# Softmax work of late batches spread over the slots, and third blocks added on TensorE, in an attention and highway kernel

## Chip, cores, metric

The kernel runs on one core of one Trainium2 chip. The metric is device time of one execution in microseconds (us). Every ratio below is the mean time of one kernel's fast runs over the mean of the other kernel's fast runs of the same rounds, with a 95% interval, so it is not quite the ratio of the medians quoted beside it.

## The reference

Linear attention for 8 batches of 8 heads, 576 rows, 64 columns; its result, as 4608 rows of 512, goes through one highway layer.

```python
q_s = softmax(q, axis=-1)              # per row
k_s = softmax(k, axis=2)               # per column
kv  = einsum('bhsd,bhse->bhde', k_s, v)
x   = einsum('bhsd,bhde->bhse', q_s, kv)   # then (4608, 512)
H = maximum(x @ w_h, 0)
T = 1 / (1 + exp(-(x @ w_t + b_t)))
out = T * H + (1 - T) * x
```

## The kernel before

Each piece of work is a small function, and a table of places (`at(place, ...)`) gives the order in which they are issued; batch c's slot has the places 8c to 8c+8. In before engines are seen to keep that order: at 67.45 us x waits 1.13 us for a query copy whose input was ready, because the copy stands behind a sum of 1.34 us on VectorE. The pieces that matter (cut):

```python
def exp_half(b, which, a):   # ScalarE: exponential of half the heads of k or q
    nc.scalar.activation(dst[b][:, :, 2*a:2*a+2, :], in32[which][b]..., AF.Exp)
def cast_v(b, a, eng=None):  # GpSimd: values to 16 bit
def q_sums(b, a):            # VectorE: row sums of half the heads, 1.34 us
def q_scale_p(b, n0, n1):    # GpSimd: queries times reciprocal of the sum
def q_trans(b, g, home=None):     # TensorE turns a third of the queries (one
    ...                           # PSUM buffer, tag "q1"); VectorE copies them
    nc.vector.tensor_copy(qsT[b][:, :, n0:n1, :], t[:, :, 0:w, :])
turned = (6, 7)              # the queries of these are turned by DMA instead
def x_pair(b, a, ...):       # TensorE: x of two of four blocks; ScalarE casts it
def gate(c, ob):             # TensorE: 4 matmuls of 512 columns, ScalarE: tanh
def carry(c, ob):            # TensorE: the same with w_h; VectorE: difference
def blend(c, ob):            # VectorE: (tanh + 1) * difference -> g

added = lambda g: ((0, 1), (0, 1, 2), (0, 1, 2), (0, 1, 2, 3))[g]
def add_x(c, ob):            # g += x for the blocks in `added`
    late = ob == (3 if c == B - 1 else 2) and c % 2 and c < B
    eng = nc.vector if late else nc.gpsimd
    eng.tensor_add(gv(ob), gv(ob), xv(ob))
def turn_block(t, k_, xs, us):   # TensorE turns g back to rows; where x was
    if xs is not None:           # not added, it is accumulated here
        mm(dst, xs, ident, True, False)
    mm(dst, us, ident, xs is None, True)
```

The pieces of softmax, kv and x of a batch b have places around `p = 8 * (b - 1)`, in slot b-1 or the one before, so that they hide between the products of batch b-1. In what follows a query turn is TensorE's transpose of a third of a batch's queries, a query copy is VectorE's copy of it out of PSUM, an x copy is ScalarE's cast of x, an output block is what `turn_block` makes, and an output copy takes it out of PSUM.

The softmax here doesn't subtract the row's maximum and nothing guards it: scores larger than these inputs give would overflow.

## Time and profile before

| | before |
|---|---|
| median of the first 3 runs | 130.17 us (129.74 to 130.88) |
| span of the profiled run | 129.5 us |
| TensorE / VectorE / ScalarE / GpSimd busy | 111.3 / 99.5 / 92.2 / 77.9 us |
| slots 3 to 7 | 13.53, 12.19, 11.81, 10.48, 8.27 us |
| first gate product after slot 7 to start of last output copy ("tail") | 12.32 us |
| start of last output copy to end of span ("end") | 4.01 us |

A slot's length is the distance between the first gate products of two following batches in the timeline. Spans are printed to 0.1 us, so an end is good to about 0.05 us. Two lines of the page of before also belong here: the clock granted to TensorE in 40 slices (9 is full speed), and the queue that brings instructions (packets, MB, share).

```profile
PEclk9999999999999999999999999999999999999998
q8 instruction: 10, 0.16, 0.5%
```

### The profile page before, as it was taken

What the parts mean: (1) busy time and instruction counts of PE and PEld (TensorE: products, weight loads), DVE (VectorE), ACT (ScalarE), POOL (GpSimd) and SP (SyncE); (2) the same over time, 40 slices, a digit from 0 to 9 for tenths busy, and PEclk for the clock granted to TensorE, in tenths of its full rate; (3) what the DMA queues carried; (4) which work ended last, traced back from release to release, by engine and by line L of the source; (5) the groups of instructions that cost most, each with busy time, mean ns of one, the idle gap of its engine ahead of it and who ended that gap; (6) DMA issues with size and microseconds to landing.
All of it is one profiled execution on the core that took longest, in us unless ns stands there. A gap on an engine that the chain in (4) does not pass through costs nothing.

```text
span 129.5 us, 3346 instructions
## 1 busy us (share of the span) xinstructions
PE 111.3 (86%) x1359; PEld 60.8 (47%) x1359; DVE 99.5 (77%) x181; ACT 92.2 (71%) x130; POOL 77.9 (60%) x73
## 2 busy tenths in 40 slices
PE   4978996986967899899769999995989999999940
PEld 2335442353424446455534555454435445579830
DVE  1297356799799999898789998983999656688960
ACT  3553049994996779679929995998797575757640
POOL 2003446690099999839964993699399746434510
PEclk9999999999999999999999999999999999999998
DMA  4999999999999999999999699999406906134994
GB/s 127 365 374 369 401 401 411 411 411 411 405 411 411 402 411 412 405 411 400 305 411 416 258 252 402 405 323 305 167 1 131 363 15 258 71 139 200 395 402 165
DMA packets 20583, 41.24 MB, mean 318 GB/s; under 512 B 5460, under 2 KB 5976, under 8 KB 19544
## 3 DMA queue, kind: packets, MB, share of 16 engines
q1 hardware_dynamic: 20568, 41.03, 85.2%
q8 instruction: 10, 0.16, 0.5%
q14 instruction: 5, 0.04, 0.1%
HBM read 30.41 MB, written 9.44 MB: 308 GB/s over the span
## 4 chain that ended last, share of the span: by engine, by line
PE 25%; DMA 20%; POOL 19%; DVE 17%; issue 7%; SPq 6%; ACT 2%; POOLq 0%; DVEq 0%; ACTq 0%
DMA v<-in_v_dram 12%; POOL eq L264 10%; DMA w32h<-in_moe_w_h_dram 8%; PE pt L64 8%; PE ph L64 8%; DVE r L234 6%; POOL v L195 4%; POOL g L421 4%; PE nat L64 4%; SPq L96 4%; DVE g L409 3%; DVE dd L401 2%; SPq L111 2%; PE psk L64 2%; PE pq L69 2%
## 5 line engine op out<-in xcount | busy, mean ns | idle before, releaser
L64 PE MATMUL pt<-xT,w16t 128*128 128x512 f16 x128 | 33.6, 379 | 2.9 <-DVE dd L401 2.1
L264 POOL TENSOR_TENSOR eq<-eq,r 128x1024 f16<-128x1024 f16 (+2 forms) x16 | 30.1, 1898 | 10.1 <-DVE r L252 10.1
L64 PE MATMUL ph<-xT,w16h 128*128 128x512 f16 x128 | 33.4, 381 | 1.3 <-ACT w16h L116 0.9
L383 ACT ACTIVATE pt<-pt,bt 128x512 f32<-128x512 f32 (+1 forms) x40 | 24.7, 621 | 7.4 <-PE pt L64 7.4
L421 POOL TENSOR_TENSOR g<-g,xT 128x512 f16<-128x512 f16 x21 | 23.9, 1151 | 8.0 <-DVE g L409 8.0
L409 DVE SCALAR_TENSOR_TENSOR g<-pt,dd 128x512 f16<-128x512 f32 (+1 forms) x40 | 25.2, 633 | 2.9
L401 DVE SCALAR_TENSOR_TENSOR dd<-xT,ph 128x512 f16<-128x512 f16 x32 | 21.7, 678 | 4.3 <-PE ph L64 4.2
L64 PEld LDWEIGHTS <-w16t 128*128 128x128 f16 x160 | 14.7, 97 | 19.1 <-issue 6.6
L183 ACT ACTIVATE eq<-q 128x1152 f16<-128x1152 f32 x16 | 18.2, 1176 | 5.4 <-DMA q<-in_q_dram 5.4
L183 ACT ACTIVATE ek<-k 128x1152 f16<-128x1152 f32 x16 | 18.6, 1175 | 1.8 <-DMA k<-in_k_dram 1.8
L195 POOL CAST v<-v 128x1152 f16<-128x1152 f32 x12 | 13.5, 1145 | 10.2 <-DMA v<-in_v_dram 10.2
L64 PEld LDWEIGHTS <-w16h 128*128 128x128 f16 x160 | 13.6, 98 | 11.7 <-ACT w16h L116 2.7
L234 DVE TENSOR_REDUCE r<-eq 128x18 f32<-128x1152 f16 x12 | 16.0, 1344 | 3.9 <-ACT eq L183 3.9
L64 PE MATMUL nat<-ident,g 128*128 128x128 f16 x142 | 16.0, 220 | 0.7 <-DVE g L409 0.4
L64 PEld LDWEIGHTS <-g 128*128 128x128 f16 x144 | 12.5, 98 | 7.6 <-DVE g L409 1.1
L461 ACT COPY o<-nat 128x512 f32<-128x512 f32 x26 | 15.6, 601 | 0.0
L354 ACT CAST xT<-px 128x1024 f16<-128x1024 f32 x10 | 10.2, 1016 | 7.6 <-PE px L64 7.6
L64 PE MATMUL warm<-wide,ident 128*128 128x512 f16 x41 | 11.9, 435 | 1.8 <-DVE wide L153 1.8
L69 PE MATMUL pq<-ident,eq 128*128 128x128 f16 x104 | 8.5, 220 | 2.7 <-DVE qsT L282 1.1
L282 DVE COPY qsT<-pq 128x1024 f16<-128x1024 f16 (+1 forms) x16 | 9.3, 587 | 1.1 <-PE pq L69 0.7
L69 PEld LDWEIGHTS <-eq 128*128 128x128 f16 x108 | 6.9, 98 | 6.0 <-issue 1.9
L357 ACT CAST xT<-px 128x512 f16<-128x512 f32 x8 | 4.3, 590 | 7.4 <-PE px L64 7.4
(57 smaller groups left out, 107.8 us busy)
## 6 DMA issues: line engine op xcount, KB each, us to landing
out_dram<-o SPq DMA_DIRECT2D x8, 1024.0 KB, 4.7
q<-in_q_dram SPq DMA_DIRECT2D x7, 1152.0 KB, 14.2
k<-in_k_dram SPq DMA_DIRECT2D x7, 1152.0 KB, 13.2
v<-in_v_dram SPq DMA_DIRECT2D x5, 1152.0 KB, 13.7
v<-in_v_dram SPq DMA_DIRECT2D x6, 576.0 KB, 11.7
q<-in_q_dram SPq DMA_DIRECT2D x2, 576.0 KB, 4.1
k<-in_k_dram SPq DMA_DIRECT2D x2, 576.0 KB, 7.2
w32t<-in_moe_w_t_dram SPq DMA_DIRECT2D x1, 1024.0 KB, 11.5
```

The lines of the kernel that those rows point to most:

```text
L64: mm = lambda o, l, r, st, sp: nc.tensor.matmul(o, l, r, start=st, stop=sp, skip_group_check=True)
L69: nc.tensor.matmul(o, i, ident, is_transpose=True, start=True, stop=True, skip_group_check=True,)
L183: nc.scalar.activation(dst[b][:, :, 2 * a : 2 * a + 2, :], in32[which][b][:, 2 * a : 2 * a + 2].rearrange("p c n d -> p n c d"), AF.Exp,)
L195: (eng or nc.gpsimd).tensor_copy(o, i)
L234: nc.vector.reduce_sum(qsum[b][:, :, h], eq[b][:, :, h, :], axis=AX.X)
L264: nc.gpsimd.tensor_mul(e, e, r.broadcast_to(list(e.shape)))
L354: copy[how](dst, t2.rearrange("p c (n d) -> p c n d", d=64))
L383: nc.scalar.activation(ps, ps, AF.Tanh, bias=bt2[:, ob : ob + 1], scale=0.5)
L401: nc.vector.scalar_tensor_tensor(dd, xv(ob), -0.5, ps, op0=ALU.mult, op1=ALU.max)
L409: nc.vector.scalar_tensor_tensor(gv(ob), th, 1.0, dd, op0=ALU.add, op1=ALU.mult)
L421: eng.tensor_add(gv(ob), gv(ob), xv(ob))
L461: nc.scalar.copy(o, flat(t))
```

## The change

The intent is to take sums and turns out of the stretch where TensorE waits for them. The query exponentials and sums of batch 5 are issued 2.3 to 3.2 places earlier, between the copies of the queries of the batch before, those of batches 6 and 7 0.2 to 1.6 places earlier; the turns of batch 5 start at the head of their slot; from batch 4 on the two halves of the values are cast one right behind the other; kv of batch 4 moves behind the last turn of its queries; the key exponentials of batch 4 come 1.3 places earlier. The third blocks of batches 2 to 5 are no longer added by GpSimd and VectorE but accumulated on TensorE, and the last addition of batch 7 goes to GpSimd.

```diff
-    added = lambda g: ((0, 1), (0, 1, 2), (0, 1, 2), (0, 1, 2, 3))[g]
+    added = lambda g: ((0, 1), (0, 1), (0, 1), (0, 1, 2, 3))[g]
...
-        late = ob == (3 if c == B - 1 else 2) and c % 2 and c < B
-        eng = nc.vector if late else nc.gpsimd
-        eng.tensor_add(gv(ob), gv(ob), xv(ob))
+        nc.gpsimd.tensor_add(gv(ob), gv(ob), xv(ob))
...
-                5: (-5, -4, -3.4, -2.7, -2.6),
-                6: (-6, -5, -3.95, -3.1, -3),
-                7: (-6, -5, -3.95, -3.1, -3),
-            }.get(b, (-5, -4, -3.9, -2.9, -2.8))
+                5: (-7.5, -6.3, -6.6, -5.5, -5.4),
+            }.get(b, (-6.6, -5.2, -5.5, -3.95, -3.9))
...
-            at(p + sc + (0.6 if b > 5 else 0), E(q_scale_p, b, 4, N9))
-            s = p + {3: 0, 4: 0}.get(b, -0.5)
-            at(s, E(exp_half, b, "k", 0), E(cast_v, b, 0))
-            at(s + 0.9, E(cast_v, b, 1))
+            at(p + sc + (0.5 if b > 5 else 0), E(q_scale_p, b, 4, N9))
+            s = p + {3: 0, 4: -1.3}.get(b, -0.5)
+            at(s, E(exp_half, b, "k", 0))
             at(s + 1, E(exp_half, b, "k", 1))
+            s = p + {3: 0, 4: 0.05, 5: 0.1}.get(b, -0.9)
+            at(s, E(cast_v, b, 0))
+            at(s + (0.9 if b == 3 else 0), E(cast_v, b, 1))
...
-            4: ((3, 4, 4.9), (4.5, 4.5), (5.9, 6.9)),
-        }.get(b, ((2, 3, 4), (4, 4), (5, 6)))
+            4: ((3, 4, 4.9), (4.95, 4.95), (5.9, 6.9)),
+        }.get(b, ((0.5, 1.6, 2.5), (4, 4), (5, 6)))
```

(The five numbers are the places of the two query exponentials, the two half sums and the scaling; then those of the three turns, of kv and of x.)

## The prediction

> **What bounds the kernel now.** I read the page first, then the list of waits, then the timeline in order, and from the built programs which instruction each wait belongs to. A slot c is the stretch in which TensorE makes the gate and carry products of batch c, four of each; softmax, kv and x of batch c+1 are woven in. Before the slots and at the end nothing is reordered except one addition, so the argument needs slots 3 to 7.
>
> ```profile
> PE 111.3 (86%) x1359; PEld 60.8 (47%) x1359; DVE 99.5 (77%) x181; ACT 92.2 (71%) x130; POOL 77.9 (60%) x73
> POOL eq L264 <- DVE r L252: 10.1, 5, 3.2
> PE psk L64 <- POOL v L195: 2.1, 4, 0.7
> PE pq L69 <- DVE qsT L282: 1.1, 3, 0.7
> ```
>
> TensorE is the fullest engine; the next lines (waiter, releaser, total us, times, longest) show its small holes: the kv sums wait for the cast values, query turns for copies on VectorE. GpSimd's 10.1 us waiting for reciprocals says that the sums come late, not that they bound.
>
> The timeline (start, duration, engine, line, what, count, idle before and its end) gives the first gate product of batches 3 to 8 at 56.89, 70.42, 82.61, 94.42, 104.90 and 113.17. So slots 3 to 7 take 13.53, 12.19, 11.81, 10.48 and 8.27 us. TensorE's own work, from starts in the timeline: four matmuls of 512 columns 0.86, an output block 0.28 (five 128-column ones) or 0.34 (six), all turns of one batch 1.0, kv 0.78, x with its ninth rows 0.80. Slot 3: 8x0.86 + 4x0.34 + 1.0 + 0.78 + 0.80 = 10.8, so 2.7 us are holes. The same sum leaves 1.6 in slot 4, 2.2 in slot 5, 0.9 in slot 6 (their output blocks have mostly five matmuls): 7.4 us in all could be had.
>
> ```profile
> 55.97 0.59 ACT L461 COPY o<-nat 128x512 f32<-128x512 f32 x1
> 56.45 1.02 ACT L354 CAST xT<-px 128x1024 f16<-128x1024 f32 x1
> 56.89 1.22 PE L64 MATMUL pt<-xT,w16t 128*128 128x512 f16 x4
> 58.15 0.66 ACT L383 ACTIVATE pt<-pt,bt 128x512 f32<-128x512 f32 x1 [0.68 <-PE pt L64]
> 59.21 2.22 ACT L183 ACTIVATE ek<-k 128x1152 f16<-128x1152 f32 x2
> ...
> 62.47 2.23 POOL L195 CAST v<-v 128x1152 f16<-128x1152 f32 x2
> ...
> 64.76 0.48 PE L64 MATMUL psk<-v,ek 64*64 64x65 f16 x36 [0.61 <-POOL v L195]
> ...
> 65.85 1.34 DVE L234 TENSOR_REDUCE r<-eq 128x18 f32<-128x1152 f16 x1
> ...
> 67.45 0.22 PE L64 MATMUL px_l<-qsT,kvn 64*64 64x64 f16 x2 [1.13 <-DVE qsT L282]
> ...
> 70.24 1.77 DVE L421 TENSOR_TENSOR g<-g,xT 128x512 f16<-128x512 f16 x1
> ```
>
> Here one sees slot 3: the second x copy starts the instant the output copy lets ScalarE go, and the gate waits for it alone; the key exponentials follow; later kv waits for values, x for a query copy that sits behind a sum; and the addition on VectorE takes 1.77 us.
>
> [...] at 67.45 x waits 1.13 us because a short copy stands behind a 1.34 us sum. [...] the addition took 1.77 and 0.77 us beside GpSimd's scaling and 0.42 us near the end, without it. [...] The query turns share one buffer, so each waits for the copy of the one before, which the 1.1 us above shows.
>
> **The change, part by part.**
>
> *Additions.* Third-block additions of batches 2 to 5 leave: two on GpSimd (1.15 each, off the path), two on VectorE (1.77 and 0.77). TensorE gets 16 more 128-column matmuls at 0.056: 0.9 us, of which 0.22 falls in slot 7, which has no holes to hide it. The last addition of batch 7 moves from VectorE to GpSimd:
>
> ```profile
> 114.16 0.69 DVE L409 SCALAR_TENSOR_TENSOR g<-pt,dd 128x512 f16<-128x512 f32 x1
> ...
> 114.89 0.42 DVE L421 TENSOR_TENSOR g<-g,xT 128x512 f16<-128x512 f16 x1
> ...
> 115.37 0.23 PE L64 MATMUL nat<-ident,g 128*128 128x128 f16 x1 [0.28 <-DVE g L421]
> ```
>
> TensorE waits for exactly this one. On GpSimd: 114.85 + 0.1 to start + 1.15 + 0.05 = 116.15 instead of 115.37, **+0.78**, with full TensorE work behind it until 121.
>
> *Slot 3.* I walk the new order with the old durations, as starts follow each other: exponential 1.06, x copy 0.90, tanh 0.58, output copy 0.48, half sum 1.26 (result visible after 1.34), reciprocal 0.30, carry difference 0.60, blend 0.61, query copy 0.60 (visible after 0.69); a product's end is seen 1.07 after its start. ScalarE now has a key exponential of batch 4 ahead of the second x copy: exponential 56.45, x copy 57.51, seen 58.53. The gate's last two matmuls go at 58.58 instead of 57.52: **first hole, 1.06 us**. ScalarE goes on: other key half 58.41, tanh 59.47, output 60.05, query exponentials of batch 5 at 60.53 and 61.59, the first seen at 61.72. VectorE has carry difference at 60.42, then must wait for that: half sum 61.77, blend 63.03, half sum 63.64, reciprocal 64.95, difference 65.25, first query copy of batch 4 at 65.85, seen 66.54. TensorE reached the second turn at 64.2 and has one buffer: it goes at 66.59, **second hole, 2.4**. It then waits for the second copy (67.2, seen 67.89): third turn 67.93, **third hole, 0.9**. kv starts 68.04; its norm is seen at 69.6; carry to 69.71; x starts 69.71 instead of 67.45; gate of batch 4 at 72.6 instead of 70.42. The values, cast by 64.70, no longer matter. With a 0.3 wait on an output copy the holes sum to 4.7: slot 3 takes 15.7, **+2.2**.
>
> *Slot 4.* The turns of batch 5 come early, their scaling (recip 65.25, GpSimd free 65.85, done 70.1) is long over, kv finds its values. Work 10.8 as in slot 3, plus 0.3 for an x copy and little else: 11.2, **-1.0**.
>
> *Slot 5.* Work 8x0.86 + 4x0.34 + 0.78 + 0.80 = 9.8. Holes: 0.3 for an x copy; ScalarE does two exponentials between tanh and output copy, so an output block waits 0.7; a half sum stands before the blend and norm: 0.3. 11.2, **-0.6**.
>
> *Slot 6.* An addition now stands between the halves of the last scaling: values of batch 7 are cast about 1 us later in the slot, kv waits 0.5: 10.7, **+0.2**. *Slot 7*: 0.22 more, **+0.2**.
>
> Sum: +2.2 - 1.0 - 0.6 + 0.2 + 0.2 + 0.78 = +1.8, that is 132.0.
>
> **The rivals.** (a) The change does what it intends: sums and turns leave the critical stretch, the value waits go. For it: 7.4 us of holes, 2.5 us off VectorE. If slot 3 fell to 11.5 as well, the sum would be 1.8 - 4.2, so about 127.8. Against it: [...] the order puts a sum that is not needed until slot 4 before products needed now. (b) The late slots tighten more than I walked: were slots 4 to 7 free of holes, 2.7 us less, 129.2; for it, half of my holes there are of 0.3 us, within the error of a walk. (c) The delay feeds itself: everything after slot 3 starts 2 us later, transposes through DMA of batch 7 start behind the later scaling, and x of slot 6 waits for them; before, they ended close to use. This would add about 1, 133. (d) A load that comes late for the earlier exponentials: batch 5's queries were issued at 40.64; with the page's median 14.2 us to landing that is 54.8, 5 us ahead of use. It is hidden.
>
> **Range and chances.** The program decides the order and the durations are measured, so I hold to the mechanism of slot 3, but small errors of a hand walk lean to (b), and a change made to a tuned kernel was made for a reason; I take 0.6 off: **131.4 us**. Range 129.4, near (b), to 133.0, (c). Faster by over 2% needs 127.6, only (a) in full: 0.07. Slower by over 2% needs 132.8: 0.14. Within 2%: 0.79.
>
> **What would show it.** Right: the gate of batch 3 with about 1 us between its second and third matmul, waiting for the x copy; in slot 3 waits of turns for query copies of about 3 us in all; first gate of batch 4 near 72.6; no kv wait for cast values in slots 3 to 5; slots 4 and 5 about 11.2 each; near the end a wait of an output block for GpSimd's addition of about 1 us. Wrong: first gate of batch 4 before 71, or VectorE's half sum of batch 5 starting before 61, which would mean that ScalarE is not the queue that holds it.

## The result, and the profile after

The changed kernel took 136.16 us (135.46 to 137.09, 4 runs), before 130.52 us (129.74 to 131.08, 4 runs): ratio 1.0441, interval 1.0345 to 1.0537. It is slower by over 4%; the prediction had given slower by over 2% a chance of 0.14, and the time lies above its range.

The page of the profile after, with the lines that answer to those of before (busy times, clock, instruction queue):

```profile
span 135.2 us, 3375 instructions
PE 114.3 (85%) x1375; PEld 62.2 (46%) x1375; DVE 97.9 (72%) x178; ACT 92.1 (68%) x130; POOL 75.7 (56%) x72
PEclk9999999999999999999856999999999999999995
q8 instruction: 11, 0.18, 0.5%
```

VectorE and GpSimd have less to do, as intended. Two things are new: the clock digits 8, 5, 6 in the middle, where slot 3 lies, and an eleventh packet of instructions. The time went to these places (each from the timelines of the two profiled runs):

| stretch | before | after | difference | predicted |
|---|---|---|---|---|
| up to slot 3 | 56.89 | 56.46 | -0.43 | 0 |
| slot 3 | 13.53 | 18.52 | +4.99 | +2.2 |
| slot 4 | 12.19 | 11.38 | -0.81 | -1.0 |
| slot 5 | 11.81 | 11.30 | -0.51 | -0.6 |
| slot 6 | 10.48 | 10.56 | +0.08 | +0.2 |
| slot 7 | 8.27 | 8.44 | +0.17 | +0.2 |
| tail | 12.32 | 13.08 | +0.76 | +0.78 |
| end | 4.01 | 5.46 | +1.45 | 0 |
| sum | 129.5 | 135.2 | +5.7 | +1.8 |

Slot 3 after, in the timeline (start, duration, engine, line, what, count, idle before and its end):

```profile
57.97 1.19 ACT L183 ACTIVATE ek<-k 128x1152 f16<-128x1152 f32 x1
58.14 0.59 PE L64 MATMUL pt<-xT,w16t 128*128 128x512 f16 x2 [1.09 <-ACT xT L354]
...
61.31 1.35 DVE L234 TENSOR_REDUCE r<-eq 128x18 f32<-128x1152 f16 x1 [0.65 <-ACT eq L183]
...
66.12 0.72 PE L69 MATMUL pq<-ident,eq 128*128 128x128 f16 x8 [2.18 <-DVE qsT L282]
67.63 0.37 PE L69 MATMUL pq<-ident,eq 128*128 128x128 f16 x2 [0.78 <-DVE qsT L282]
...
69.07 1.89 PE L64 MATMUL ph<-xT,w16h 128*128 128x512 f16 x4
...
71.56 1.88 PE L64 MATMUL pt<-xT,w16t 128*128 128x512 f16 x4
```

The first five lines are the three holes that the prediction had walked: 1.09, 2.18 and 0.78 us, with the causes it named. The last two are not in it: four matmuls of 512 columns take 1.89 us and not 1.03. The windows view says why (us, then busy time and count of TensorE, its weight loads, VectorE, ScalarE and GpSimd, then granted clock, DMA share, GB/s):

```profile
63.07:66.48 3.41, 1.08 (x15) 0.73 (x13) 3.38 (x6) 1.49 (x3) 3.41 (x4) 1.00 0.91 284
...
64.00:66.00 2.00, 0.00 (x0) 0.00 (x0) 1.97 (x5) 0.56 (x1) 2.00 (x3) 1.00 0.87 299
66.50:68.00 1.50, 0.72 (x11) 0.36 (x11) 0.86 (x2) 0.00 (x0) 1.50 (x2) 0.50 1.05 412
68.00:70.00 2.00, 2.00 (x76) 1.38 (x76) 0.90 (x3) 0.00 (x0) 2.00 (x2) 0.50 1.04 411
70.00:72.00 2.00, 2.00 (x13) 0.45 (x12) 0.91 (x2) 0.32 (x1) 2.00 (x3) 0.50 1.04 410
72.00:73.20 1.20, 1.20 (x4) 0.42 (x3) 0.48 (x1) 0.70 (x1) 0.89 (x1) 0.50 1.03 407
```

The clock was halved (0.50) from about 66.5 to 73.3 us, 6.8 us, right after the hole of 2.18 us. No stretch of full idleness as long as 3.41 us came before it: TensorE was still 1.08 us busy in the 3.41 us before the fall. How much idleness it took in the traces is said under "Open".

At the other end, the wait list of the DMA queue's engine and the timeline for the last store (its issue, then the final wait), first before:

```profile
126.09 0.41 SPq L497 DMA_DIRECT2D out_dram<-o  x1
SPq L647 <- DMA out_dram<-o: 1.9, 1, 1.9
```

and after:

```profile
130.34 1.14 SPq L495 DMA_DIRECT2D out_dram<-o  x1
SPq L645 <- DMA out_dram<-o: 2.6, 1, 2.6
```

The issue takes 0.73 us longer and the wait 0.7: that is the longer end, +1.45 by the rounded spans and +1.37 by the traces' own time stamps. The eleventh instruction packet, 16 KB, starts at 130.2 us, just ahead of that issue, and takes 0.9 us. In before the tenth and last was at 113.1.

The third, small loss is where the prediction had it:

```profile
118.43 1.15 POOL L419 TENSOR_TENSOR g<-g,xT 128x512 f16<-128x512 f16 x1 [0.91 <-DVE g L409]
...
119.63 0.23 PE L64 MATMUL nat<-ident,g 128*128 128x128 f16 x1 [0.99 <-POOL g L419]
```

### The profile page after: what moved, and what is told of

Its sections match the earlier page's. It is cut to its first block, busy times and chain, and to the rows that moved or that the text cites.

```text
span 135.2 us, 3375 instructions
## 1 busy us (share of the span) xinstructions
PE 114.3 (85%) x1375; PEld 62.2 (46%) x1375; DVE 97.9 (72%) x178; ACT 92.1 (68%) x130; POOL 75.7 (56%) x72
## 4 chain that ended last, share of the span: by engine, by line
PE 33%; POOL 17%; DVE 13%; DMA 11%; ACT 8%; issue 7%; SPq 7%; DVEq 0%; POOLq 0%; ACTq 0%
PE ph L64 11%; PE pt L64 10%; POOL eq L264 8%; DMA w32h<-in_moe_w_h_dram 8%; POOL g L419 5%; PE nat L64 4%; SPq L96 3%; DVE dd L401 3%; DMA qsD<-eq 3%; SPq L111 3%; DVE g L409 3%; PE pq L69 3%; POOL v L195 2%; PE psk L64 2%; PE px L64 2%
## 5 line engine op out<-in xcount | busy, mean ns | idle before, releaser
L64 PE MATMUL pt<-xT,w16t 128*128 128x512 f16 x128 | 34.8, 387 | 3.1 <-DVE dd L401 1.2
L64 PE MATMUL ph<-xT,w16h 128*128 128x512 f16 x128 | 34.2, 388 | 1.1 <-ACT w16h L116 0.7
L419 POOL TENSOR_TENSOR g<-g,xT 128x512 f16<-128x512 f16 x20 | 22.9, 1154 | 14.0 <-DVE qsT L282 7.4
L64 PE MATMUL nat<-ident,g 128*128 128x128 f16 x142 | 16.9, 219 | 2.1 <-POOL g L419 1.0
L64 PEld LDWEIGHTS <-g 128*128 128x128 f16 x144 | 13.2, 98 | 9.6 <-issue 1.8
```

The lines of the kernel that those rows point to most:

```text
L64: mm = lambda o, l, r, st, sp: nc.tensor.matmul(o, l, r, start=st, stop=sp, skip_group_check=True)
L419: nc.gpsimd.tensor_add(gv(ob), gv(ob), xv(ob))
```

## The experiments

All kernels gave correct results. The slots of their profiled runs, in us:

| kernel | 3 | 4 | 5 | 6 | 7 | tail | end | median us (runs) | ratio to before |
|---|---|---|---|---|---|---|---|---|---|
| before | 13.53 | 12.19 | 11.81 | 10.48 | 8.27 | 12.32 | 4.01 | 130.17 to 130.92 | 1 |
| before, second trace | 13.60 | 12.18 | 11.81 | 10.47 | 8.27 | 12.32 | 4.03 | 131.59 (1) | - |
| after | 18.52 | 11.38 | 11.30 | 10.56 | 8.44 | 13.08 | 5.46 | 136.16 (4) | 1.0441 |
| e1 last addition back | 18.51 | 11.38 | 11.34 | 10.53 | 8.44 | 12.31 | 5.09 | 135.62 (4) | 1.0326 |
| e2 keys of 4 back (profile slow) | 18.02 | 11.37 | 14.71 | 10.07 | 8.44 | 13.08 | 5.53 | 137.09 (4) | 1.0389 |
| e3 sums, turns of 5 back | 13.39 | 12.34 | 11.18 | 10.70 | 8.44 | 13.07 | 5.19 | 133.17 (4) | 1.0160 |
| e5 after, hole filled | 15.90 | 11.37 | 11.29 | 12.23 | 8.44 | 13.07 | 5.42 | 135.29 (4) | 1.0335 |
| e6 additions alone (profile slow) | 13.61 | 11.73 | 14.09 | 10.07 | 8.44 | 12.32 | 5.45 | 133.62 (4) | 1.0159 |
| e7 e3 with keys and last addition back | 12.37 | 12.34 | 11.17 | 10.70 | 8.44 | 12.32 | 5.46 | 131.08 (20) | 1.0040 |
| e8 slot 3 reordered | 13.18 | 11.48 | 11.25 | 10.63 | 8.45 | 12.31 | 5.54 | 131.08 (20) | 1.0031 |
| e10 before, padded | 13.62 | 12.18 | 11.81 | 10.57 | 8.27 | 12.31 | 5.32 | 132.85 (4) | 1.0164 |
| e11 e7, fewer rows | 12.38 | 12.33 | 11.18 | 10.70 | 8.44 | 12.32 | 4.09 | 129.92 (4) | 0.9914 |
| e12 e11, turns of 5 earlier | 12.36 | 11.48 | 11.35 | 10.52 | 8.44 | 12.32 | 4.03 | 129.00 (4) | 0.9849 |
| e13 as e12, rows saved otherwise | 12.37 | 11.48 | 11.80 | 10.68 | 8.28 | 12.32 | 4.08 | 128.78 (4) | 0.9837 |

In two profiles (e2, e6) the run was slow: slot 5 of those two had a clock of 0.88, and its length is not used. The traces show what that was: a clock of 0.50 for 3.41 us (from 95.54 in e2, from 92.08 in e6), close to the end of a wait of 2.04 and 2.10 us of x of batch 6 for its transpose by DMA.

**e1: the last addition back on VectorE.** Otherwise the changed kernel.

```diff
-        nc.gpsimd.tensor_add(gv(ob), gv(ob), xv(ob))
+        eng = nc.vector if (c, ob) == (B - 1, 3) else nc.gpsimd
+        eng.tensor_add(gv(ob), gv(ob), xv(ob))
```

> The changed kernel with one thing undone: the last addition of batch 7 goes back from GpSimd to VectorE. If that addition stood on the path (the step of +0.78 us in the prediction), the wait of 0.99 us of an output block for it near the end shrinks to about 0.28 us and the kernel is 0.7 to 0.8 us faster than the changed one, about 135.4 us. If the end is set by the last store instead, nothing changes.

Measured: the tail is 12.31 instead of 13.08, 0.77 less, and no slot moves. The time is 135.62 us, ratio 1.0326 (1.0249 to 1.0402). The cost of that one addition is settled by the trace; the two ratios' intervals overlap.

**e2: the key exponentials of batch 4 back.** Otherwise the changed kernel.

```diff
-            s = p + {3: 0, 4: -1.3}.get(b, -0.5)
+            s = p + {3: 0, 4: 0}.get(b, -0.5)
```

> The changed kernel with the key exponentials of batch 4 back behind the second x copy. If the holes of slot 3 add up one by one, the first hole (1.1 us) goes and the kernel is 1 us faster. My walk says otherwise: VectorE's chain (half sums of batch 5, then the copy that a query turn waits for) is the bound of slot 3, the query exponentials come no earlier, so the hole only moves behind: the gate of batch 3 has no wait, the wait of the second turn grows from 2.2 to about 3.2 us, the clock falls as before, and the time stays within 0.5 us of the changed kernel, 135.5 to 136.5 us.

Measured: slot 3 still takes 18.02 us, and the clock falls there too (0.81 in the mean of the slot). The 1.09 us hole at the gate is gone, but its time comes back as a wait of 1.97 us for an output copy and 1.38 for a query copy. The holes do not add: VectorE's row of sum, blend, sum, reciprocal, difference, copy stands between. The ratio is 1.0389 (1.0315 to 1.0462).

**e3: sums and turns of batch 5 back.** Otherwise the changed kernel.

```diff
-                5: (-7.5, -6.3, -6.6, -5.5, -5.4),
+                5: (-5, -4, -3.4, -2.7, -2.6),
...
-        }.get(b, ((0.5, 1.6, 2.5), (4, 4), (5, 6)))
+        }.get(b, ((2, 3, 4), (4, 4), (5, 6)))
```

> The changed kernel with the query exponentials, sums, scaling and turns of batch 5 at their old places; everything else stays changed. Theory (the sums of batch 5 ahead of the query copies of batch 4 make the holes and with them the clock drop): the waits of the turns in slot 3 fall under 1 us, the granted clock stays at 1.00 through slots 3 to 7, slot 3 takes 13 to 14 us instead of 18.5 and the kernel about 131 us. Rival (the keys in front of the x copy, the casts, or the extra matmuls make the loss): it stays above 134 us.

Measured: slot 3 falls from 18.52 to 13.39 us, the clock stays at 1.00 all through the slots, slot 4 is back at 12.34. Ratio 1.0160 (1.0091 to 1.0229). So the early sums of batch 5, with their exponentials, are what opens the large hole, as the prediction said, and with the hole goes the fall of the clock. The expected time of about 131 us was missed: the tail (13.07) and the end (5.19) stay those of after.

**e5: the hole filled.** The changed kernel with nine matmuls on zeros where the hole begins; they shorten nothing.

```diff
+    def fill_hole(n):
+        t = two_banks("fill")[:, 0]
+        for _ in range(n):
+            mm(t, ident, wide, True, True)
...
+        if b == 4:
+            at(p + 4, E(fill_hole, 9))
```

> The changed kernel with nine idle matmuls of 512 columns (1.94 us in all) put into the hole ahead of the second query turn of batch 4, into a bank that is free there; they compute nothing that is used and wait for nothing late. They cannot shorten any wait. If the fall of the granted clock to 0.50 after this hole costs the 2.8 us that my walk of slot 3 lacked, the clock stays at 1.00, slot 3 takes 15.5 to 16 us instead of 18.5, and the kernel 133 to 133.5 us. If the 2.8 us come from something else (the waits themselves being longer), the time stays or grows.

In the timeline the fillers take the place of the hole, and the products after it have their full speed again:

```profile
63.29 2.11 PE L64 MATMUL fill<-wide,ident 128*128 128x512 f16 x9
65.64 0.61 PE L69 MATMUL pq<-ident,eq 128*128 128x128 f16 x8 [0.24 <-DVE qsT L287]
67.93 1.04 PE L64 MATMUL ph<-xT,w16h 128*128 128x512 f16 x4
...
69.30 1.04 PE L64 MATMUL pt<-xT,w16t 128*128 128x512 f16 x4
```

Slot 3 takes 15.90 us, 2.62 less than after, with more work in it. That is the experiment that separates the two: the waits alone make 15.90 (the walk had 15.7), the clock makes the rest. The second turn starts 9.66 us after the first gate product in both kernels, so the fillers lengthen nothing. The expected 133 to 133.5 us were missed: the whole time is hardly better than after, 135.29 us, ratio 1.0335 (1.0268 to 1.0402); in the trace it is slot 6 that takes most of the gain back, with 12.23 instead of 10.56: x of batch 7 waits there 1.57 us, to 103.79. The profile names a blend of VectorE as what it waited for, but the second transpose by DMA, issued at 98.6 and landing 5.2 us later, ends there. That is rival (c) of the prediction; in after x waited only 0.2 us for a transpose.

**e6: the third blocks on TensorE and nothing else.** From before; the last addition stays on VectorE.

```diff
-    added = lambda g: ((0, 1), (0, 1, 2), (0, 1, 2), (0, 1, 2, 3))[g]
+    added = lambda g: ((0, 1), (0, 1), (0, 1), (0, 1, 2, 3))[g]
```

> The kernel before with the additions part alone: third blocks of batches 2 to 5 added on TensorE, no addition on VectorE. Theory (this part costs 0.78 us near the end and 0.2 us in slot 7, and gives back some tenths in slots 4 and 6 where VectorE's additions stood before products): within 1 us of the kernel before, 130.5 to 131.7 us, no fall of the clock in slots 3 to 7. Rival (the extra matmuls carry the loss): 133 us or more.

Measured: slot 3 is unchanged at 13.61, slot 4 gains 0.46 (11.73), and the end is 5.45 instead of 4.01. So the longer end comes with this part, and not with the spreading. The ratio of the two fast runs is 1.0159 (1.0039 to 1.0278), which leaves open how much it costs; the expected 130.5 to 131.7 us holds one of the two. The profile is a slow one, so its time in sum is not compared.

**e7 and e8: two other orders of slot 3**, with a second run of before (e9) beside them. Both keep the third blocks on TensorE, the casts as changed, the later kv of batch 4, and the early sums of batches 6 and 7; the last addition is on VectorE.

```diff
# e7: the edits of e1, e2 and e3 together
# e8: the edit of e1, and
-                5: (-7.5, -6.3, -6.6, -5.5, -5.4),
+                5: (-7.5, -3.5, -4.95, -2.9, -2.85),
...
-            s = p + {3: 0, 4: -1.3}.get(b, -0.5)
+            s = p + {3: 0, 4: 0.6}.get(b, -0.5)
...
-            at(s + 1, E(exp_half, b, "k", 1))
+            at(s + (1.9 if b == 4 else 1), E(exp_half, b, "k", 1))
...
-        }.get(b, ((0.5, 1.6, 2.5), (4, 4), (5, 6)))
+        }.get(b, ((1.6, 2.5, 3.5), (4, 4), (5, 6)))
```

> The changed kernel with all of slot 3 undone: key exponentials of batch 4, and query exponentials, sums, scaling and turns of batch 5 at their old places; the last addition on VectorE. What remains of the change is the later casts, batches 6 and 7, and the third blocks. Theory: slot 3 at or a little under the 13.4 us of the run with the sums alone undone, slots 5 to 7 as in the changed kernel, about 130 to 131 us, so the same as before within 1%. If the spreading of batches 6 and 7 were what costs, it stays above 133 us.

> A better order by the same reasoning, last addition on VectorE: the first query exponential of batch 5 ahead of the key exponentials of batch 4 but behind the second x copy; its first half sum only after the first query copy of batch 4, its second after the kv norm and a carry difference; turns of batch 5 a little later in slot 4. My walk gives slot 3 about 12.3 us and slot 4 about 11.6, the rest as in the changed kernel without the last addition: about 129 to 130 us, 0.5 to 1.5% faster than before. If VectorE has no slack in slot 3 whatever the order, it stays at 130.5 or more.

> The kernel before once more, for a second trace: whether its time from the last output copy to the end of the span is again 4.0 us, against 5.1 to 5.5 us in the five kernels of the changed kind, or whether that differs from run to run; and whether its slots 3 to 7 repeat within 0.3 us (13.5, 12.2, 11.8, 10.5, 8.3).

Measured: e7's slot 3 is 12.37, 1.16 less than before's; the timeline shows kv of batch 4 behind the last turn and without a wait for values (before waited 0.61 us for them, and 1.13 for the last query copy). e8's slot 3 is 13.18 where 12.3 was expected, and its time 131.08 us where 129 to 130 was: its half sum of batch 5 stands ahead of the second query copy, and the third turn waits for it:

```profile
64.78 0.27 PE L69 MATMUL pq<-ident,eq 128*128 128x128 f16 x2 [1.72 <-DVE qsT L282]
```

The clock stayed at 1.00 through that hole of 1.72 us. Over 20 runs, 18 of them fast, both come out a little slower than before: 1.0040 (1.0015 to 1.0065) and 1.0031 (1.0002 to 1.0060), although their slots 3 to 7 and the tail sum to 1.3 us less for e7 (67.34 against 68.60) and 1.3 for e8 (67.30). What eats this is the end: 5.46 and 5.54 us. The second trace of before has 4.03, so it is no chance of one trace.

**e10: the end, tested on before.** All traces with the long end had eleven instruction packets, and all had the 16 additional matmuls with their 16 weight loads. To tell the packet from the additions, I put 16 small matmuls into the warm-up of before.

```diff
+    def pad(n):
+        for _ in range(n):
+            mm(warm[:, 0:64], ident, wide[:, 0:64], True, True)
...
-        E(warm_up, 24),
+        E(warm_up, 24), E(pad, 16),
```

> The kernel before with 16 small matmuls (64 columns) added to the warm-up at its start: 32 more rows in TensorE's stream, as many as the change adds, and no other change. Theory (the end of 1.1 to 1.5 us is an instruction fetch of 16 KB that TensorE's longer stream calls for just as the last store runs): the page counts 11 packets on the instruction queue instead of 10, the eleventh within the last 6 us, the stretch from the last output copy to the end of the span is 5.1 to 5.5 us instead of 4.0, and the time rises by 0.8 to 1.4 us; slots 3 to 7 stay 13.5, 12.2, 11.8, 10.5, 8.3. Rival (the end is longer because the additions on TensorE change the order of the last copies and stores): 4.0 us and no change of the time, whatever the number of fetches.

The page of before padded, and the last store:

```profile
PE 114.1 (86%) x1375; PEld 62.0 (47%) x1375; DVE 100.3 (76%) x181; ACT 92.4 (70%) x130; POOL 77.9 (59%) x73
PEclk9999999689999999999999999999999999999995
q8 instruction: 11, 0.18, 0.5%
127.89 0.66 SPq L501 DMA_DIRECT2D out_dram<-o  x1
SPq L651 <- DMA out_dram<-o: 2.9, 1, 2.9
```

Slots 3 to 7 and the tail are before's within 0.1 us, and the end is 5.32 instead of 4.01. So work that has nothing to do with additions, stores or the end lengthens the end, if it only makes the stream longer. In each of the nine traces with eleven packets the last one starts within 0.6 us of the start of the last output copy; in the five with ten it lies over 12 us ahead of it. The ratio is 1.0164 (1.0102 to 1.0226): about 2.1 us, of which the end explains 1.3. In the profiled run the slots also begin 1.6 us later, with a clock of 0.50 from 23.99 to 27.40 us (the digits 6 and 8); what the unprofiled runs lost beyond 1.3 is not settled.

**e11: the reverse.** e7 with 8 matmuls fewer in the warm-up.

```diff
-        E(warm_up, 24),
+        E(warm_up, 16),
```

> The kernel with keys of 4, sums and turns of 5 and the last addition put back as before (131.08 us in the earlier run), with 8 warm-up matmuls less at the start, so 16 rows less in TensorE's stream. Theory of the fetch: 10 packets on the instruction queue, 4.0 us from the last output copy to the end instead of 5.46, and 129.6 to 130.1 us, a ratio to before of 0.993 to 0.997. Rival: 5.46 us stays, and the time too, a ratio of 1.004. [...]

Measured: ten packets again; the end 4.09, no slot moved; 129.92 us, ratio 0.9914 (0.9879 to 0.9949), where e7 had 1.0040. The DMA view of the last three stores (out, in, KB, us to landing) shows that it is the landing that differs; before padded:

```profile
out_dram<-o SPq DMA_DIRECT2D x1, 512.0 KB, 5.1
out_dram<-o SPq DMA_DIRECT2D x1, 384.0 KB, 3.8
out_dram<-o SPq DMA_DIRECT2D x1, 128.0 KB, 3.7
```

and fewer rows:

```profile
out_dram<-o SPq DMA_DIRECT2D x1, 512.0 KB, 3.3
out_dram<-o SPq DMA_DIRECT2D x1, 384.0 KB, 2.4
out_dram<-o SPq DMA_DIRECT2D x1, 128.0 KB, 2.4
```

The windows view (its last two numbers are DMA share and GB/s) shows where the landing is lost, before padded first, fewer rows second:

```profile
130.00:131.18 1.18, 0.00 (x0) 0.00 (x0) 0.00 (x0) 0.00 (x0) 0.00 (x0) 0.50 0.07 23
126.87:128.40 1.53, 0.00 (x0) 0.00 (x0) 0.00 (x0) 0.00 (x0) 0.00 (x0) 0.50 0.01 5
```

Before padded, a share of 0.07, by estimate one of 16 engines, is still at work for over 1 us after the others have done; with fewer rows next to nothing is. So about one DMA engine ends its part of the last stores late. That it is the one that carried the instructions is likely, not shown.

**e12 and e13: the better versions.** e12 is e11 with the turns of batch 5 at 1.6, 2.5, 3.5 instead of 2, 3, 4. e13 has these turns too, the whole warm-up, and saves its rows by giving the third blocks of batches 4 and 5 back to GpSimd and VectorE.

```diff
# both, from e7
-        }.get(b, ((2, 3, 4), (4, 4), (5, 6)))
+        }.get(b, ((1.6, 2.5, 3.5), (4, 4), (5, 6)))
# e12: warm_up 16.  e13 instead:
-    added = lambda g: ((0, 1), (0, 1), (0, 1), (0, 1, 2, 3))[g]
+    added = lambda g: ((0, 1), (0, 1), (0, 1, 2), (0, 1, 2, 3))[g]
...
-        eng = nc.vector if (c, ob) == (B - 1, 3) else nc.gpsimd
+        late = (c, ob) in ((5, 2), (B - 1, 3))
+        eng = nc.vector if late else nc.gpsimd
```

> As the run with fewer rows, and the turns of batch 5 half a step earlier in slot 4 than before the change (1.6, 2.5, 3.5 instead of 2, 3, 4). Slot 4 falls from 12.34 to about 11.5, the other slots stay at 12.4, 11.2, 10.7, 8.4, 12.3, the end is 4.0: 128.8 to 129.4 us, ratio 0.986 to 0.991. If the shorter slot 4 is given back in slot 5 or 6 (x of batch 6 or 7 waiting for a transfer), no gain over the run with fewer rows.

> As the last, but the 16 rows are saved by leaving the third blocks of batches 4 and 5 to GpSimd and VectorE as before the change, with the warm-up whole. Theory of the fetch: again 10 packets and an end of 4.0. Slot 5 gets VectorE's addition (about 1 us) back and is 11.2 to 11.8: 128.8 to 130 us, ratio 0.987 to 0.996. If only the shorter warm-up and not the row count ended the fetch, 11 packets and an end of 5.1 to 5.5.

Measured: slot 4 is 11.48 in both; both have ten packets and an end of 4.03 and 4.08; 129.00 us, ratio 0.9849 (0.9810 to 0.9888), and 128.78 us, ratio 0.9837 (0.9795 to 0.9879). e13 has the warm-up of before and 1367 matmuls, like e11 and e12 (ten packets; eleven with 1375 in after and e10), so it is the length of the stream that decides, not the warm-up. Both are faster than before, by 1.5 and 1.6%, with intervals clear of 1, though not by 2%.

## Why the prediction was wrong

**Right: the holes of slot 3.** "First hole, 1.06 us" was 1.09; the "second hole, 2.4" was 2.18; the "third hole, 0.9" was 0.78. VectorE's half sum, walked to 61.77, began at 61.31, in a run whose slot 3 began 0.43 earlier. That this comes from the early sums of batch 5 is shown by e3, and e5 gives the waits' own length of slot 3: 15.90 for a predicted 15.7.

**Wrong: "I walk the new order with the old durations, as starts follow each other".** Old durations hold only at the old clock: four matmuls of 512 columns took 1.03 us at 1.00 and 1.89 us at 0.50. The prediction saw three holes one behind the other, 4.7 us of idle TensorE in one slot, and never asked what they do to the clock. The products behind the holes ran at half speed for 6.8 us, and slot 3 took 18.52. The missing term is 18.52 - 15.90 = 2.62 us. Its check "first gate of batch 4 near 72.6" failed: 74.98.

**Wrong: the sum stops at the tail.** "Sum: +2.2 - 1.0 - 0.6 + 0.2 + 0.2 + 0.78" has no term for the stores, taken as unchanged. The 16 matmuls were counted as 0.9 us of TensorE time, hidden but for 0.22, and not as 32 more instructions. That cost about 1.4 us in after; e10 and e11 show it from both sides. The eleventh packet of 16 KB is not hidden: the end is 5.46 us in after and 5.32 in e10, with eleven, and 4.01 in before, with ten.

**Right: the rest.** Slot 4 (-0.81 for -1.0), slot 5 (-0.51 for -0.6), slots 6 and 7, and the last addition (+0.76 for +0.78; e1: 0.77). No kv product waited for values in slots 3 to 5. The 0.43 us gained before slot 3 were not foreseen: 0.28 of them lie in slot 2 (11.94 for 12.22), as in e6 (11.95), so these come with the third blocks.

**The rivals.** (a), no loss in slot 3, did not come about in the change, though e7 shows that slot 3 could have fallen to 12.37 with another order. (b), hole-free late slots, did not. (c), the DMA transposes that come too late, is real but lay at the edge: 0.2 us in after, 1.57 us in e5, about 2 in the slow profiles of e2 and e6. (d), the late load, did not: the query exponentials of batch 5 did not wait for it in after. Of the +5.7 us of the profiled runs, the steps of the walk make +2.1 (slot 3 at 15.90: +2.37 - 0.81 - 0.51 + 0.08 + 0.17 + 0.76), the clock +2.62, the end +1.45, and the start -0.43. The range, made of rivals that are all waits, could not hold two terms that are none. The 0.6 us taken off the walk's 132.0 moved the number the wrong way.

**Open.** What exactly makes the clock fall. It fell in slot 3 of after and e1, with a hole of 2.18 us in each, and did not in e8 with 1.72. The record says more than that. In after the clock falls at 66.47 us, rises at 73.30 and falls again at 131.32, which is 2 and 17 steps of 3.41 us; in e2 its two falls in the slots, at 64.82 and 95.54, lie 9 such steps apart. The falls go with how busy TensorE was in the step before. Here are the step ahead of the fall in after, the one with the hole of e8, and the emptiest of before's slots:

```profile
63.06:66.47 3.41, 1.08 (x15) 0.72 (x13) 3.38 (x6) 1.50 (x3) 3.41 (x4) 1.00 0.90 283
62.09:65.51 3.42, 1.70 (x81) 1.45 (x83) 2.93 (x5) 3.16 (x4) 3.42 (x5) 1.00 0.97 350
63.67:67.08 3.41, 2.04 (x78) 1.25 (x78) 2.30 (x4) 2.01 (x3) 3.26 (x3) 1.00 0.96 378
```

At full clock the steps with 0.96 us of TensorE work (e2), 1.08 (after), 1.31 (e6) and 1.59 (e2) were followed by half clock; those with 1.70 (e8) and 2.04 (before) were not, the one with 1.98 in e10 was (the profiles of e2 and e6 are slow ones). So a hole need not fill a step, and where the steps happen to lie may count too. In e3 and e7 no stretch of 3.41 us in slots 3 to 7, wherever laid, has less than 2.3 us of work, so their full clock is no luck of that kind; the same holds for e5's slot 3. This is read from traces that were made for something else; no run moved a hole within a step to test it.

The profiled run of after is the slowest of its four, and single profiles give the parts of the +5.7. Unprofiled runs of after had mean clocks of 0.961, 0.978 and 0.983 for before's 0.99 or so, so the low stretch is likely not equally long in each; only the profiled run shows where it lies. Also, the packet alone, about 0.9 us on one of the DMA engines (5.5% of 16 engines' time in the one us from 130), is shorter than the 1.3 to 1.4 us it costs.

## What to carry to other kernels

Before accepting a reorder that leaves TensorE with several idle stretches one behind the other, add up how busy it stays over any 3.4 us (the step seen here, in which 1.08 and 1.59 us were too little) and read the granted clock around them: what follows may run at half speed, as it did here for 6.8 us (clock 0.50), and a filler of useless matmuls tells the wait from the clock in one run. Count instructions as well as microseconds: 32 more in TensorE's stream (e10) brought one more instruction packet, eleven for ten, just as the last store went out, and the end went from 4.01 to 5.32 us; taking 16 away from e7 gave it back, 4.09 us for 5.46. Where a kernel stands is read from the instruction queue's packets. When a change mixes parts, undo each alone: here what was left in e13 made the kernel 1.6% faster than before once the bad parts were gone. Of that, the turns of batch 5 are shown to be worth 0.85 us in slot 4 (e11 against e12); the later kv of batch 4, the casts and the sums of batches 6 and 7 were not run apart.
